# A chunked attention with two dense layers behind it: loads with 2 MB under way, one state sum moved, marks for two banks

## The chip, the cores and the metric

The kernel runs on one core of a Trainium2 chip. The metric is the device time of one execution in microseconds (us). Names of engines: PE is TensorE's matmul side, PEld its weight loads, DVE is VectorE, ACT is ScalarE, POOL is GpSimd, SP is SyncE, which here only issues transfers. One profiled execution of the kernel before is shown; other executions were only timed.

## The reference

A linear attention with decay (2 batches, 8 heads, 768 positions in 12 blocks of 64, head size 64), a dense layer pair with a leaky rectifier (1536 tokens, 512 to 2048 to 512), and a second pair (512 to 1024 to 512) with a softmax-weighted activation and a layer norm.

```python
for b in range(12):                                   # blocks of 64
    intra = (q_b @ k_b.T * Dmask) @ v_b
    inter = (q_b * lam_pow) @ kv_state
    out_b = intra + inter
    kv_state = lam_block * kv_state + (k_b * rev_pow).T @ v_b
x = out                                               # (1536, 512)
h = x @ w_in;  x = maximum(0.01 * h, h) @ w_out
h = x @ w_in2; s = h * softmax(h)
return (layernorm(s) * g_ln) @ w_out2
```

## The kernel before

**Numbers.** Weights come as 8-byte words, 512 KB a tile of 128 x 512 (`raww`). ACT and DVE turn each into two fp32r parts, a high one and a low one (`wio`): `word_hi` and `word_lo` on ACT (L351, L355), `clamp`, `shift`, `join` on DVE (L361, L371, L380), `high` on ACT (L410), `low` on DVE (L429). A product of two such numbers is three matmuls: high by high, high by low, low by high.

**Stages.** A prologue does attention steps 0 to 3 for the first 512 tokens, in products of 64 x 64. Then 48 units follow, 16 for each of three blocks of 512 tokens. Unit u makes 128 hidden columns (`l1_mm`, L440, 12 matmuls of 512 columns into a bank `hps`), ACT and DVE split them (`l1_split`: L443, L446, and `glo` L448 on DVE), and `l2_mm` (L457, 12 matmuls) adds them to `acc` one unit later. During the first 16 units the weights of the units to come are loaded and converted, one pair (a tile of `w_in` and a tile of `w_out`) for each unit; n counts pairs from 0. Steps 4 to 11 of the attention stand inside units 7, 10, 12, 14, 17, 21, 25 and 29. The second layer pair ends the kernel.

**A step.** `scores_mm` (L197) and `scores_ev` (L205, `r` on DVE) make the masked scores, `xs_mm` (L251) and `xq_mm` (L265) the output, `state_mm` (L211) the new sum for the state into bank `kb` (= `aps[1]`), `state_ev` (L237, or four instructions at L226) adds it on DVE to the decayed state. `x_hi` (L300, ACT) and `x_lo` (L304, DVE) split a step's output into `xhi` and `xlo`, which `l1_mm` reads. Steps of the prologue have the other half of rows than steps 4 to 11 have. In step 3, `xq_mm` goes ahead of `xs_mm`; `see` writes to the bank and has ACT copy one column of it, and the first `xs_mm` of each batch waits for that copy.

**Order.** Each engine runs its instructions in the order in which the code writes them; a pass at the end of the kernel fixes that. SP issues the loads in that order too. `load` adds one more wait: with `limit` bytes under way or more, a load waits for an earlier one. `AHEAD` is 2 MB, `CALM` 1 MB.

Of the kernel before, what the change touches and what calls it, by code (L numbers as in the profile page):

```python
# [10 lines left out]
U32 = mybir.dt.uint32  # L11
# [5 lines left out]
P = 128  # L17
CH = 64
NPAIR = 4
NB = 2  # L20
NPRE = 4
# [3 lines left out]
AHEAD, CALM = 1 << 21, 1 << 20  # L25
# [3 lines left out]
NF = FF1 // P  # L29
# [15 lines left out]
def fused_kernel(ctx: ExitStack, tc: tile.TileContext, att, vt, tab, cst, w_in, w_out, w_in2, w_out2, out):  # L45
# [7 lines left out]
    pe, dve, act, pool, sync = nc.tensor, nc.vector, nc.scalar, nc.gpsimd, nc.sync  # L53
# [10 lines left out]
    aps = [pp.tile([P, 512], F32, name=f"aps{i}") for i in range(2)]  # L64
# [19 lines left out]
    def rows(h):  # L84

        return HALF[1 - h]

    def jrows(s, h):

        return HALF[h] if s < NPRE else HALF[1 - h]  # L90
# [5 lines left out]
    def at(bank, rows, b, pr):  # L96

        if isinstance(bank, tuple):
            return bank[b][rows, pr * CH : (pr + 1) * CH]
        return bank[rows, (b * NPAIR + pr) * CH : (b * NPAIR + pr + 1) * CH]  # L100
# [12 lines left out]
    def load(queue, out, in_, limit=AHEAD):  # L113

        size = 4
        for n in out.shape:
            size *= n
        ins = queue.dma_start(out=out, in_=in_).ins
        ahead = size
        for before, n in reversed(flight):  # L120
            ahead += n
            if ahead > limit:
                tc.add_manual_dep(ins, before.name, SYNC, reason="bytes under way")
                break
        flight.append((ins, size))
# [67 lines left out]
    def scores_mm(s, bank, b, pr):  # L193
        q, k = (qk_t[s][:, :, 0], qk_t[s][:, :, 1]) if s >= NPRE else ld[s][0:2]
        for h in range(2):
            d = rows(h)
            pe.matmul(at(bank, jrows(s, h), b, pr), k[d, b, pr], q[d, b, pr], start=True, stop=True)  # L197
# [41 lines left out]
    LASTPRE, seen, mark = NPRE - 1, {}, tabs[:, 0:NB]  # L239

    def see(s, b):
        c = (b * NPAIR + NPAIR) * CH - 1
        bank = (aps, hps)[b][0]
        scores_mm(s, bank, b, NPAIR - 1)
        seen[b] = act.copy(mark[:, b : b + 1], bank[:, c : c + 1]).ins

    def xs_mm(s, bank, b, pr):
# [27 lines left out]
    def each_pair(*groups):  # L275

        for pr in range(NPAIR):
            for mm, s, bank, b in groups:
                mm(s, bank, b, pr)

    def alone(mm, s, bank):
        for b in range(NB):
            each_pair((mm, s, bank, b))

    def both(mm, s, bank, mm2, s2, bank2):
        for b in range(NB):
            each_pair((mm, s, bank, b), *([(mm2, s2, bank2, b)] if s2 < NS else []))

    def step(s, xbank, kbank, rbank):

        both(xs_mm, s, xbank, state_mm, s if s < NS - 1 else NS, kbank)
        both(xq_mm, s, xbank, scores_mm, s + 1, rbank)
# [5 lines left out]
    def x_hi(s, bank):  # L298
        for src, dst in parts(bank, x_place(s, xhi)):
            act.copy(dst, src)  # L300

    def x_lo(s, bank):
        for src, dst, hi in parts(bank, x_place(s, xlo), x_place(s, xhi)):
            dve.tensor_tensor(dst, src, hi.bitcast(F32), op=ALU.subtract)  # L304
# [8 lines left out]
    def whole(n):  # L313

        return IN if n == 0 else OUT if n == NF else BOTH

    def load_weights(n, halves=None):
        if n >= len(order):
            return
        kind, f = order[n]  # L320
        if n not in raws:
            if n == NF:
                raws[n] = tmp.tile([P, 1, 512, 2], U32, tag="s", name="rawl")
            else:
                raws[n] = wp.tile([P, 2, 512, 2], U32, tag="w", name="raww")
        t = raws[n]
        if kind == "a":
            load(sync, out=t.rearrange("p h a b -> p (h a b)"), in_=w_in2[f].bitcast(U32))
            return
        halves = halves or whole(n)  # L330
        for i in range(halves.start, halves.stop):
            src = w_out2[f + i] if kind == "b" else w_out[f - 1] if i else w_in[f]
            load(sync, out=t[:, 0 if n == NF else i].rearrange("p a b -> p (a b)"), in_=src.bitcast(U32), limit=AHEAD if n + i < 2 else CALM // 2 if n == 1 else CALM)

    def of(n, halves):

# [38 lines left out]
    def join(n, halves=None):  # L375
        if n >= len(order):
            return
        raw, x = of(n, halves)
        xu = x.bitcast(U32)
        dve.scalar_tensor_tensor(xu, xu, 0x80000000, raw[:, :, 0], op0=ALU.bitwise_and, op1=ALU.bitwise_or)  # L380
# [19 lines left out]
    def high(n, halves=None):  # L400
        if n >= len(order):
            return
        kind, f = order[n]
        halves = halves or whole(n)
        t, x = pieces(n), xs_t[n]
        if kind == "b":
            for i in range(2):
                act.activation(t[:, 0, i], x[:, i], AF.Copy, scale=gln[:, f + i : f + i + 1])
        else:
            act.copy(t[:, 0, halves], x[:, halves])  # L410
# [23 lines left out]
    def l1_mm(u, bank):  # L434
        b, f = u
        w = win_t[f].rearrange("p s (k c) -> p s k c", k=KD)
        groups = ((0, xhi), (1, xhi), (0, xlo)) if u == (0, 0) else ((0, xhi), (0, xlo), (1, xhi))
        terms = [(s, k, x) for s, x in groups for k in range(KD)]
        for i, (s, k, x) in enumerate(terms):
            pe.matmul(bank, w[:, s, k], x[b][:, k], start=(i == 0), stop=(i == len(terms) - 1))  # L440
# [136 lines left out]
    c1 = nc.const_aps.tensor(1.0, (P, 1), BF16)  # L577
# [3 lines left out]
    def busy(n):  # L581
        for _ in range(n):
            pe.matmul(aps[0], c1.to_broadcast([P, P]), c1.to_broadcast([P, 512]), start=True, stop=True)
# [29 lines left out]
    xb, sb, kb = acc[0:2], acc[2:4], aps[1]  # L613
# [47 lines left out]
    x3 = (xb[1], hps[1])  # L661
    for b in range(NB):
        each_pair((xq_mm, 3, x3, b))
        see(3, b)
    join(1, IN)
    x_lo(2, xb[0])
    both(xs_mm, 3, x3, state_mm, 3, kb)
    busy(1)
    x_hi(3, x3)
    high(1, IN)  # L670
    x_lo(3, x3)
# [42 lines left out]
    for i, u in enumerate(items[1:], 1):  # L714
        bank = hps[i % 2]
        s = step_at.get(i)
        spare = hps[(i + 1) % 2]
        if i > 1:
            if i == 5:
                alone(scores_mm, NPRE, aps[0])  # L720
            l1_mm(u, bank)
            if s is not None:
                step(s, aps[0], aps[1], spare)
        if i == 2:
            join(3, IN)
            high(3, IN)
            clamp(3, OUT)
            low(3, IN)
            shift(3, OUT)
            l1_split(u, bank)  # L730
            words(4, IN)
            join(3, OUT)
            high(3, OUT)
            clamp(4, IN)
            shift(4, IN)
            low(3, OUT)
            words(4, OUT)
            join(4, IN)
            high(4, IN)
            clamp(4, OUT)  # L740
            shift(4, OUT)
            low(4, IN)
            word_hi(5)
            join(4, OUT)
            word_lo(5)
        elif i == len(items) - 1:
            h2_norm(1, second=lambda: l1_split(u, bank))
        elif i > 2:
            part = OUT if i == 3 else None
            high(pair_at(i, 1), part)  # L750
            clamp(pair_at(i, 2))
            shift(pair_at(i, 2))
            low(pair_at(i, 1), part)
            l1_split(u, bank)
            if s is not None:
                scores_ev(s + 1, spare)
            if i == 6:
                scores_ev(NPRE, aps[0])
                scale_q(NPRE, pool)
                scale_k(NPRE, act)  # L760
            if s is not None:
                state_ev(s, aps[1])
                x_hi(s, aps[0])
                x_lo(s, aps[0])
                load_kv(s + 1)
                load_qk(s + 2)
                scale_q(s + 1, pool)
                decay_state(s + 1, pool)
            if i - 1 in step_at:
                scale_k(step_at[i - 1] + 1, act)  # L770
            join(pair_at(i, 2))
            if i == 4:
                state_ev(NPRE - 1, kb)
            words(pair_at(i, 3))
        load_weights(pair_at(i, 5))
        if i == 2:
            load_kv(NPRE)
            load(sync, out=fix, in_=cst)
            load_qk(NPRE + 1)
        if i == len(items) - 3:  # L780
            h2_norm(0)
            ln_turn(0, on_act=())
        l2_mm(items[i - 1])
        if items[i - 1][1] == NF - 1:
            l2_split(items[i - 1][0])
        if i in h2_after:
            h2_mm(h2_after[i])
# [84 lines left out]
```

## Time and profile before

| | us |
|---|---|
| median of 3 timed executions | 445.64 |
| lowest, highest of them | 443.67, 447.14 |
| the profiled execution's own time | 448.04 |
| its span, first to last instruction | 446.3 |
| PE busy, DVE busy, ACT busy | 435.1, 266.6, 196.1 |

The span is what the rows count in. The profiled execution's own time is 1.7 above it, and 2.4 above the median of the timed ones. Busy time of PE counts matmuls that overlap once.

### The profile page before, as it was taken

The numbers are of one execution on the slowest core, as the hardware profiler recorded it, in microseconds if no ns is written. First come the engines' busy times: TensorE is split into PE (matmuls) and PEld (weight loads), VectorE is DVE, ScalarE is ACT, GpSimd is POOL, SyncE is SP. The second block draws the span as 40 slices with busy tenths as digits, with TensorE's granted clock in tenths as the row PEclk, the third lists the DMA queues.
The fourth block names the chain that finished last, engine by engine and source line by source line (L and its number), as shares of the span: only waits on it lengthen the run. The fifth ranks groups of instructions, "written<-read, shape, count | busy, mean of one in ns | idle before, by whom it ended". The sixth has DMA issues, their size and how long they took to land.

```text
span 446.3 us, 8024 instructions
## 1 busy us (share of the span) xinstructions
PE 435.1 (97%) x3270; PEld 358.0 (80%) x3272; DVE 266.6 (60%) x423; ACT 196.1 (44%) x332; POOL 31.4 (7%) x38
## 2 busy tenths in 40 slices
PE   9779998999999999999999999999999999999996
PEld 4668887888888888888888888888888888888886
DVE  4769989999632121211132888707779877777640
ACT  3558976977452232221244778612423322222221
POOL 0600102022202020100000000000000000000000
PEclk9989999999999999999999999999999999999999
DMA  8757877864303030100015552000112222222111
GB/s 286 288 195 237 242 255 239 262 189 144 96 2 96 0 95 1 48 1 0 1 51 198 209 196 101 0 1 7 41 34 62 95 76 73 75 73 74 58 47 47
DMA packets 23699, 46.85 MB, mean 105 GB/s; under 512 B 4336, under 2 KB 12016, under 8 KB 23152
## 3 DMA queue, kind: packets, MB, share of 16 engines
q1 hardware_dynamic: 21792, 44.78, 30.9%
q10 hardware_dynamic: 1872, 1.58, 1.3%
q8 instruction: 25, 0.41, 0.4%
q14 instruction: 10, 0.08, 0.1%
HBM read 37.95 MB, written 3.15 MB: 92 GB/s over the span
## 4 chain that ended last, share of the span: by engine, by line
PE 83%; ACT 0%; issue 0%; DVE 0%
PE acc L457 25%; PE hps L440 24%; PE acc L569 15%; PE aps L477 6%; PE hps L477 5%; PE acc L477 4%; PE aps L251 1%; PE aps L265 1%; PE hps L197 0%; PE aps L211 0%; PE aps L537 0%; PE acc L537 0%; ACT osb L572 0%; DVE state L226 0%
## 5 line engine op out<-in xcount | busy, mean ns | idle before, releaser
L440 PE MATMUL hps<-xhi,wio 128*128 128x512 f32 x384 | 104.3, 394 | 1.6 <-DVE r L205 1.2
L448 DVE TENSOR_TENSOR glo<-hps,ghi 128x512 fp32r<-128x512 f32 x48 | 33.1, 690 | 111.8 <-ACT ghi L446 111.7
L457 PE MATMUL acc<-ghi,wio 128*128 128x512 f32 x384 | 95.9, 392 | 0.0
L440 PEld LDWEIGHTS hps<-xhi,wio 128*128 128x128 f32 x384 | 72.9, 191 | 17.1 <-ACT raww L355 1.5
L457 PEld LDWEIGHTS acc<-ghi,wio 128*128 128x128 f32 x384 | 71.4, 188 | 15.1
L443 ACT ACTIVATE hps<-hps 128x512 f32<-128x512 f32 x48 | 28.0, 584 | 105.7 <-PE hps L440 105.7
L569 PE MATMUL acc<-wb,ln 128*128 128x512 f32 (+1 forms) x312 | 67.6, 373 | 0.0
L569 PEld LDWEIGHTS acc<-wb,ln 128*128 128x128 f32 x312 | 55.3, 188 | 10.2
L440 PE MATMUL hps<-xlo,wio 128*128 128x512 f32 x192 | 51.3, 389 | 0.0
L457 PE MATMUL acc<-glo,wio 128*128 128x512 f32 x192 | 51.3, 389 | 0.0
L440 PEld LDWEIGHTS hps<-xlo,wio 128*128 128x128 f32 x192 | 36.0, 188 | 7.6
L457 PEld LDWEIGHTS acc<-glo,wio 128*128 128x128 f32 x192 | 36.0, 188 | 7.5
L380 DVE SCALAR_TENSOR_TENSOR x<-x,raww 128x1024 uint32<-128x1024 uint32 (+1 forms) x28 | 31.8, 1134 | 0.1
L351 ACT ACTIVATE x<-raww 128x1024 f32<-128x1024 f32 (+1 forms) x28 | 27.9, 996 | 8.5 <-DMA raww<-in_w_in_dram 5.2
L371 DVE SCALAR_TENSOR_TENSOR raww<-x,raww 128x1024 uint32<-128x1024 uint32 (+1 forms) x28 | 29.6, 1056 | 3.3 <-ACT raww L355 1.0
L446 ACT CAST ghi<-hps 128x512 fp32r<-128x512 f32 x48 | 28.2, 587 | 1.5
L355 ACT ACTIVATE raww<-raww 128x1024 uint32<-128x1024 uint16 (+1 forms) x28 | 28.1, 1003 | 0.0
L429 DVE TENSOR_TENSOR wio<-x,wio 128x1024 fp32r<-128x1024 f32 (+1 forms) x21 | 22.0, 1049 | 1.8 <-ACT wio L410 1.7
L510 POOL TENSOR_TENSOR small<-small,nhalf 128x1 f32<-128x1 f32 x12 | 6.6, 549 | 234.5 <-DVE small L509 234.5
L410 ACT CAST wio<-x 128x1024 fp32r<-128x1024 f32 (+1 forms) x21 | 17.8, 847 | 11.1 <-DVE x L380 11.1
L572 ACT COPY osb<-acc 128x512 f32<-128x512 f32 (+1 forms) x13 | 7.2, 554 | 32.0 <-PE acc L569 19.5
L166 POOL TENSOR_TENSOR qk<-qk,qpow 128x512 f32<-128x512 f32 x8 | 10.8, 1345 | 143.4 <-PE hps L197 109.0
(115 smaller groups left out, 496.1 us busy)
## 6 DMA issues: line engine op xcount, KB each, us to landing
raww<-in_w_out_dram SPq DMA_DIRECT2D x23, 512.0 KB, 4.2
raww<-in_w_in_dram SPq DMA_DIRECT2D x16, 512.0 KB, 4.4
qk<-in_att_dram SPq DMA_DIRECT2D x8, 512.0 KB, 4.6
raww<-in_w_in_dram SPq DMA_DIRECT2D x4, 1024.0 KB, 4.8
lt<-e SPq DMA_DIRECT2D x124, 32.0 KB, 1.8
out_dram<-osb SPq DMA_DIRECT2D x11, 256.0 KB, 2.2
ldw<-in_att_dram SPq DMA_DIRECT2D x7, 384.0 KB, 5.2
kv<-in_att_dram SPq DMA_DIRECT2D x16, 128.0 KB, 3.4
```

The costliest lines, as they stand in the source:

```text
L351: act.activation(x, raw[:, :, 1].bitcast(F32), AF.Copy, scale=HI_SCALE)
L355: act.activation(raw[:, :, 0], raw.bitcast(U16)[:, :, 1], AF.Copy, scale=LO_SCALE)
L371: dve.scalar_tensor_tensor(raw[:, :, 0], x.bitcast(U32), 3, raw[:, :, 0], op0=ALU.logical_shift_left, op1=ALU.bitwise_or)
L380: dve.scalar_tensor_tensor(xu, xu, 0x80000000, raw[:, :, 0], op0=ALU.bitwise_and, op1=ALU.bitwise_or)
L429: dve.tensor_tensor(t[:, 1, halves], x[:, halves], t[:, 0, halves].bitcast(F32), op=ALU.subtract)
L440: pe.matmul(bank, w[:, s, k], x[b][:, k], start=(i == 0), stop=(i == len(terms) - 1))
L443: act.activation(bank, bank, AF.Prelu, alpha=0.01)
L446: act.copy(ghi, bank)
L448: dve.tensor_tensor(glo, bank, ghi.bitcast(F32), op=ALU.subtract)
L457: pe.matmul(acc[m], w[:, s, m], g, start=(f == 0 and first), stop=(f == NF - 1 and last))
L477: pe.matmul(bank, x[b][:, k, o : o + P], w2_t["a", k, half][:, s], start=(i == 0), stop=(i == len(terms) - 1),)
L569: pe.matmul(po[:, 0:n], x[:, k], w2_t["b", k][:, s, cols], start=(i == 0), stop=(i == len(terms) - 1))
```

## The change

Three things change, and nothing in the order of the loads.

Weight loads from pair 3 on (the fourth) have the limit of 2 MB in place of 1 MB; pair 1 keeps 2 MB for its first tile and 512 KB for its second, pair 2 keeps 1 MB.

`state_mm` of step 3 leaves the prologue, where it alternated with `xs_mm`, and alternates with `scores_mm` of step 4 in unit 5; its `state_ev` goes from unit 4's row of the loop to unit 6's. A filler matmul (`busy(1)`) behind it goes.

`see` writes its mark by one bf16 matmul of 64 columns of ones, where it computed two products of scores before; the copied column is another one.

```diff
     def see(s, b):
-        c = (b * NPAIR + NPAIR) * CH - 1
+        c = CH - 1
         bank = (aps, hps)[b][0]
-        scores_mm(s, bank, b, NPAIR - 1)
+        pe.matmul(bank[:, 0:CH], c1.to_broadcast([P, P]), c1.to_broadcast([P, CH]), start=True, stop=True)
         seen[b] = act.copy(mark[:, b : b + 1], bank[:, c : c + 1]).ins
...
-            load(sync, out=t[:, 0 if n == NF else i].rearrange("p a b -> p (a b)"), in_=src.bitcast(U32), limit=AHEAD if n + i < 2 else CALM // 2 if n == 1 else CALM)
+            load(sync, out=t[:, 0 if n == NF else i].rearrange("p a b -> p (a b)"), in_=src.bitcast(U32), limit=CALM // 2 if n == 1 and i else CALM if n == 2 else AHEAD)
...
     x_lo(2, xb[0])
-    both(xs_mm, 3, x3, state_mm, 3, kb)
-    busy(1)
+    alone(xs_mm, 3, x3)
     x_hi(3, x3)
...
             if i == 5:
-                alone(scores_mm, NPRE, aps[0])
+                both(scores_mm, NPRE, aps[0], state_mm, NPRE - 1, kb)
...
-            if i == 4:
+            if i == 6:
                 state_ev(NPRE - 1, kb)
```

On PE, at the end of the prologue, the 16 state products (`aps_86<-ldw`) and the filler went from between step 3's output products (`acc_80` and `hps_84` `<-r,ldw`) and the first matmuls of unit 0:

```order
-L251 MATMUL hps_84<-r,ldw 64x64 x2
-L211 MATMUL aps_86<-ldw 64x64 x2
-L583 LDWEIGHTS const-bfloat16-1.0
-L583 MATMUL aps_85<-const-bfloat16-1.0 128x512
+L244 LDWEIGHTS const-bfloat16-1.0
+L244 MATMUL hps_83<-const-bfloat16-1.0 128x64
+L251 MATMUL acc_80<-r,ldw 64x64 x8
+L251 MATMUL hps_84<-r,ldw 64x64 x8
 L440 MATMUL hps_83<-xhi_95,wio 128x512 x8
```

Unit 0 now follows step 3's 16 output products at once; the products that left stand in unit 5.

On DVE, in unit 6, the addition of step 3's state comes behind `join` (L380) of pair 8, where it came behind that of pair 6 before:

```order
 L205 TENSOR_TENSOR r<-aps_85,dmask 128x512
 L380 SCALAR_TENSOR_TENSOR x<-x,raww 128x1024
+L237 TENSOR_TENSOR state<-aps_86,sd 128x512
 L361 TENSOR_SCALAR x<-x 128x1024
 L371 SCALAR_TENSOR_TENSOR raww<-x,raww 128x1024
```

It is now the last thing on DVE ahead of unit 7, whose step 4 reads that state.

On SP, from the second tile of pair 2 (`raww_141`) over pair 3 (`raww_144`) and step 4's `qk` to pair 4 (`raww_149`); the names in brackets are semaphores of earlier transfers. Before:

```order
L118 DMA raww_141<-in_w_out_dram 128x1024 [waits DMAHW7_49]
L118 DMA raww_144<-in_w_in_dram 128x1024 [waits DMAHW2_49,DMAHW0_49]
L118 DMA raww_144<-in_w_out_dram 128x1024 [waits DMAHW3_49,DMAHW1_49]
L118 DMA qk_147<-in_att_dram 128x2x512 [waits DMAHW4_49]
L118 DMA raww_149<-in_w_in_dram 128x1024 [waits DMAHW5_49,DMAHW3_49]
```

And after the change:

```order
L118 DMA raww_141<-in_w_out_dram 128x1024 [waits DMAHW7_49]
L118 DMA raww_144<-in_w_in_dram 128x1024 [waits DMAHW2_49]
L118 DMA raww_144<-in_w_out_dram 128x1024 [waits DMAHW3_49]
L118 DMA qk_147<-in_att_dram 128x2x512 [waits DMAHW4_49,DMAHW0_49]
L118 DMA raww_149<-in_w_in_dram 128x1024 [waits DMAHW5_49,DMAHW1_49]
```

The loads stand in one order in both; what moved is which landing each waits for, two transfers further back.

## Rows read from the trace of the kernel before

**Rows 1.** The page: the chain's shares by engine, and the DMA rate by fortieths.

```profile
PE 83%; ACT 0%; issue 0%; DVE 0%
...
GB/s 286 288 195 237 242 255 239 262 189 144 96 2 96 0 95 1 48 1 0 1 51 198 209 196 101 0 1 7 41 34 62 95 76 73 75 73 74 58 47 47
```

**Rows 2.** Waits of PE: who waited for whom, us in total, times, longest.

```profile
PE aps L211 <- issue: 2.4, 1, 2.4
PE hps L440 <- DVE r L205: 1.2, 1, 1.2
```

**Rows 3.** Stretches: PE, PEld, DVE, ACT, POOL busy (x instructions), clock, DMA, GB/s.

```profile
13.62:19.00 5.38, 3.11 (x128) 2.97 (x127) 3.63 (x6) 3.75 (x11) 4.39 (x4) 1.00 0.61 238
19.00:25.20 6.20, 3.53 (x127) 3.40 (x128) 4.50 (x7) 2.21 (x6) 0.61 (x1) 1.00 0.82 264
...
26.30:29.70 3.40, 3.14 (x7) 2.49 (x8) 2.90 (x6) 3.07 (x7) 0.00 (x0) 0.50 0.79 270
...
26.56:72.72 46.16, 46.16 (x340) 37.58 (x340) 42.53 (x58) 38.98 (x59) 2.98 (x2) 0.97 0.73 234
73.87:110.00 36.13, 36.13 (x396) 29.96 (x397) 34.58 (x41) 27.11 (x40) 5.79 (x5) 1.00 0.70 209
```

**Rows 4.** Timeline of PE, prologue to unit 8: start, length, instruction, wait.

```profile
16.34 0.27 PE L251 MATMUL acc<-r,ldw 64*64 64x64 f32 x2
...
17.34 0.40 PE L197 MATMUL acc<-ldw 64*64 64x64 f32 x7
19.47 0.97 PE L197 MATMUL acc<-ldw 64*64 64x64 f32 x25 [1.73 <-issue]
...
25.40 0.21 PE L211 MATMUL aps<-ldw 64*64 64x64 f32 x1 [2.40 <-issue]
...
26.56 3.55 PE L440 MATMUL hps<-xhi,wio 128*128 128x512 f32 x8 [0.42 <-ACT xhi L300]
29.94 1.09 PE L440 MATMUL hps<-xlo,wio 128*128 128x512 f32 x4
30.87 1.09 PE L440 MATMUL hps<-xhi,wio 128*128 128x512 f32 x4
...
52.74 1.15 PE L197 MATMUL aps<-qk 64*64 64x64 f32 x32
...
67.67 0.27 PE L251 MATMUL aps<-r,kv 64*64 64x64 f32 x2
...
69.70 2.11 PE L457 MATMUL acc<-ghi,wio 128*128 128x512 f32 x8
...
73.87 1.15 PE L440 MATMUL hps<-xhi,wio 128*128 128x512 f32 x4 [1.16 <-DVE r L205]
```

**Rows 5.** Timeline of ACT.

```profile
26.13 0.37 ACT L300 CAST xhi<-hps 128x256 fp32r<-128x256 f32 x1 [2.79 <-PE hps L251]
...
31.13 0.58 ACT L443 ACTIVATE hps<-hps 128x512 f32<-128x512 f32 x1 [0.83 <-PE hps L440]
...
61.46 1.14 ACT L351 ACTIVATE x<-raww 128x1024 f32<-128x1024 f32 x1 [2.70 <-DMA raww<-in_w_out_dram]
```

**Rows 6.** Timeline of DVE.

```profile
32.36 0.69 DVE L448 TENSOR_TENSOR glo<-hps,ghi 128x512 fp32r<-128x512 f32 x1 [0.99 <-ACT ghi L446]
...
62.64 0.70 DVE L361 TENSOR_SCALAR x<-x 128x1024 f32<-128x1024 f32 x1 [0.74 <-ACT x L351]
63.67 1.23 DVE L371 SCALAR_TENSOR_TENSOR raww<-x,raww 128x1024 uint32<-128x1024 uint32 x1 [0.34 <-ACT raww L355]
...
67.14 1.22 DVE L380 SCALAR_TENSOR_TENSOR x<-x,raww 128x1024 uint32<-128x1024 uint32 x1
...
73.05 0.68 DVE L205 TENSOR_TENSOR r<-hps,dmask 128x512 f32<-128x512 f32 x1
```

**Rows 7.** The tile of step 3's state on DVE, in unit 4's row.

```profile
L237 DVE TENSOR_TENSOR state<-aps,sd x1: 677/677/677, 56.4 to 56.4; 128x512 f32<-128x512 f32 x1
```

**Rows 8.** Timeline of SP: the issue of pair 3's first tile.

```profile
23.62 0.33 SPq L118 DMA_DIRECT2D raww<-in_w_in_dram  x1
```

## The prediction

> **What bounds the kernel now.** I began with the chain that ended last: 83% of the span lies on PE and next to nothing on ACT, DVE or issue [rows 1]. The stretches then say where PE has no gap: from 26.56, the first matmul of unit 0, to 72.72 it is busy 46.16 of 46.16 us, and from 73.87 to 110.00 again 36.13 of 36.13 [rows 3]. So ahead of 110 an edit can move the end in three ways: unit 0 starts earlier, the wait between 72.72 and 73.87 gets shorter, or a stretch of the clock changes. The list of PE's waits names them [rows 2]: 2.4 us with no releaser ahead of a state product in the prologue, and 1.2 us for DVE's `r` ahead of unit 8.
>
> The first is the more telling. On the timeline PE stops at 17.74 (17.34 and 0.40) until 19.47, and at 23.00 until 25.40, with nothing that it waits for [rows 4]. Between the ends of one pause and the start of the next stand 128 matmuls and as many weight loads, give or take one [rows 3]: 256 instructions. Pauses that stand a fixed count of instructions apart, whatever the instructions are, are waits for code. I treat them so: the pause belongs to the 256th instruction, and the block of code behind it came 5.93 us after PE had gone on from the last pause (19.47 to 25.40). A 64 x 64 product in fp32 is two matmuls there, so the narrow products of the prologue use code up fast: 32 products in 1.0 us (16.34 to 17.34).
>
> The pause costs more than itself. PE had done almost nothing from 23.00 to 25.40, and from 26.30 to 29.70 the granted clock is 0.50, that is 1.2 GHz in place of 2.4 [rows 3]: the first eight matmuls of unit 0 take 3.38 us (26.56 to 29.94), the next four 0.93 [rows 4].
>
> Next I asked what sets the second wait. DVE's `r` ran at 73.05 [rows 6], and DVE is busy 42.53 of 46.16 us up to there [rows 3]: it is nearly the bound itself. Its waits on the way are 0.99 ahead of `glo` of unit 0, where ACT had waited 0.83 for the slow matmuls, and 0.74 and 0.34 ahead of pair 8's conversion, where ACT had waited 2.70 for that pair's second tile [rows 5, 6].
>
> **The change, part by part.** *The state products leave the prologue.* From the pause's end at 19.47 the code now runs 25 matmuls of step 3's scores, 32 and 32 of `xq_mm` for steps 2 and 3, 2 marks, 32 of `xs_mm`: 123. The 128th is the fifth of unit 0. Ahead of unit 0 the pause is gone. `x_hi` of step 3's second batch ran at 26.13, having waited 2.79 for these products [rows 5]; less 2.40, and less about 0.1 for the marks, which are one matmul each for four, it runs at 23.6, and unit 0 starts at 26.56 - 2.5 = 24.05. Worth 2.5. The 16 products take nothing else with them: alternating with the output products they ran beside those (32 in 1.0 us, where 16 alone take about 1.1 at 52.74) [rows 4]. The filler stood in `x_hi`'s time, so it was free and stays so.
>
> *In unit 5* they alternate with the scores of step 4. Bounds: nothing, by the alternating row, to 1.15, the length of such 16 alone [rows 4]. I take 0, the row that has the same pairing.
>
> *The pause in its new place.* Five matmuls at 0.23 end at 25.2; if the block comes when it came, at 25.40, PE stands 0.2. The other seven end at 27.0, at the full clock, since PE now works in most of the stretch in which it stood still. Before, those twelve ended at 30.87. PE is 3.87 ahead.
>
> The Trainium skill, "Runtime: NRT & Kernel Launch", section "Instruction fetch mechanics", has engines read code in blocks of 256 instructions, the next while the last runs, and calls the cost of crossing "mostly hidden". The count agrees with the trace, the cost does not: 1.73 and 2.40 us stand open here. By the page the pause would be something else and might stay; the rival for that is below.
>
> *DVE and ACT.* Both run up to unit 0's split in the order that they had, 2.5 earlier. ACT would be free for it at 31.13 - 0.83 - 2.5 = 27.8, and PE has ended at 27.0, so the 0.83 goes and `glo` comes 3.3 earlier, at 29.05.
>
> *2 MB under way.* The wait at 61.46 was for the second tile of pair 8. From pair 3's first tile to that one SP issues twelve tiles of 0.52 MB, `qk` twice, `kv` and a small table: 7.9 MB. The first two fortieths, with 2 MB under way, moved 286 and 288 GB/s, the fourth to eighth 237 to 262 [rows 1]. From 23.62, where pair 3 was issued [rows 8] (it goes a little earlier now), 7.9 MB are through at 51.3 by the first rate and at 57 by the lowest of the second. ACT wants the tile at 58.76 - 3.3 = 55.5. By the first rate nobody waits; by the second ACT waits 1.5, less than the 1.62 that DVE did not feel of the 2.70. So DVE's 0.74 + 0.34 = 1.08 goes in both. The ends: 0 to 1.08; I take 1.08. Durations on ACT and DVE I leave as they are.
>
> *The addition of step 3's state* is 0.68 on DVE [rows 7] and stands ahead of `r` of unit 7 in both kernels, so the sum up to `r` is the same. But step 4's state products need its bank and its result. `join` of pair 8 ran at 67.14 [rows 6]; 4.4 earlier it ends at about 63.9 and the addition at 64.5, while PE reaches step 4 at 67.67 - 3.87 = 63.8. PE stands 0.7 there, with the rest of the step and `l2_mm` of unit 6 queued behind. The step itself takes 2.03 (67.67 to 69.70) [rows 4]. That is covered: PE has to wait for `r` behind them anyway. Without that cover it costs 0.7. On POOL and SP the move issues nothing. The tile with step 3's `k` and `v` is held until unit 5; the load that takes it over is that of pair 12, seven pairs on.
>
> *The sum.* DVE's `r` of unit 7 comes 3.3 + 1.08 = 4.4 earlier, and unit 8 starts at 69.5 in place of 73.87. PE alone would be there at 72.72 - 3.87 = 68.8, or 69.5 with the wait in step 4, so DVE still decides, by little, and half of the 1.16 stays. Behind unit 8 PE and DVE stand to each other as before, with the loads not later. 448.04 - 4.4 = 443.6 for an execution like the profiled one.
>
> That one lies above all three timed ones (443.67 to 447.14), which differ by 3.5 with nothing changed. What varies is most likely what this sum removes: a faster execution may not have had the slow clock or the wait for pair 8. So I count 2.5 for the pause in full, and half of the other 1.9 against the median: 445.64 - 3.45 = 442.2. The measurement tells about 1% from no change, which is 441.2 on this side and 450.1 on the other.
>
> **The rivals.**
>
> *The pause comes back inside unit 0.* The third block is read under more loads than before. If it comes at 26.9, 7.4 us after the last pause, PE stands 1.7 again and the clock may fall again: seven matmuls at 0.42 end at 29.85, `glo` (1.49 behind, as 30.87 to 32.36) at 31.3, a gain of 1.0, and 1.08 with it: 445.64 - 2.1 = 443.6, between 443.1 and 445. For it: 5.93 us was under 264 GB/s, and the five matmuls cover only 1.2. Against: the loads that come early are issued behind 22, and the block was due before they weigh much.
>
> *More than the sum.* If DVE drops out of the way, PE alone gives 3.87 + 1.16 = 5.0: 440.6. For it: DVE is only 0.7 behind PE in the sum. Against: step 4's new wait for the addition.
>
> *Slower: code behind 2 MB of loads.* If the block's time grows with the bytes under way, PE stands in unit 0 far longer. It decides from 29.0 on: seven matmuls at 0.42 end at 31.95, `glo` at 33.44, which eats the 1.08. With twice 5.93 the block comes at 31.3 and the gain turns into a loss of 2.3: 447.9. Over 1% takes 33.5. Against: only the third block is in reach; the next falls 128 wide matmuls later.
> The Trainium skill, "DMA: Bandwidth & Descriptors", section "Queues, rings and completion order", has each DMA engine take turns between queues packet by packet; by that code would not stand behind all the loads. No row here shows single packets.
>
> *It does not do what it says.* If the pauses are not code, the pause stays where it is in the program's time, and only 0 to 1.08 is gained: 444.6 to 445.6.
>
> **How the numbers follow.** Forecast 0.44 (441.2 to 443.1 for gains of 2.5 to 4.4), pause back 0.26, more 0.17, no effect 0.07, slower 0.06. The range runs from 440.6, PE alone, to 445.0, the end of the first rival; outside lie half of "more", most of "no effect" and "slower", less than 0.2. Faster by over 1%: "more" and the edge of the forecast, 0.30. Slower by over 1%: 0.04 (half of that rival and what I do not see). Within 1%: 0.66.
>
> **What would show it.** Right: no pause ahead of step 3's `x_hi`; unit 0 at about 24.0; a pause, short, ahead of its fifth matmul; granted clock 1.00 through unit 0; no wait of ACT for a weight tile behind 30; unit 8 at about 69.5. Wrong: a pause of over 1 us in unit 0, a stretch at 0.50 there, unit 8 later than 71.5, or a wait of over 1 us in step 4.

## The result, and the profile after

The changed kernel takes 442.36 us (median of 16, 441.44 to 443.50), the kernel before 446.08 in the same series (16, 443.67 to 449.08): a ratio of 0.9916, 95% interval 0.9895 to 0.9936. The forecast was 442.2, and the measured time lies in the range. The spread shrank too, from 5.4 to 2.1.

The profiled execution took 441.71, its span 439.9. PE's timeline, to be held against [rows 4]:

```profile
17.94 0.97 PE L197 MATMUL acc<-ldw 64*64 64x64 f32 x25 [1.10 <-issue]
18.69 1.61 PE L265 MATMUL acc<-qs,state 64*64 64x64 f32 x48
20.24 0.20 PE L244 MATMUL aps<-const-bfloat16-1.0 128*128 128x64 bf16 x1
...
21.63 0.63 PE L251 MATMUL hps<-r,ldw 64*64 64x64 f32 x16
...
22.74 2.11 PE L440 MATMUL hps<-xhi,wio 128*128 128x512 f32 x8 [0.47 <-ACT xhi L300]
24.68 1.07 PE L440 MATMUL hps<-xlo,wio 128*128 128x512 f32 x4
25.59 1.07 PE L440 MATMUL hps<-xhi,wio 128*128 128x512 f32 x4
...
64.75 2.11 PE L457 MATMUL acc<-ghi,wio 128*128 128x512 f32 x8
...
67.60 1.07 PE L440 MATMUL hps<-xhi,wio 128*128 128x512 f32 x4
```

Ahead of unit 0 PE waits only 0.47 for `xhi`, as it waited 0.42 before; there is no pause without a releaser there, none inside unit 0, and no wait ahead of unit 8. The stretches (columns as in [rows 3]) say the same, and that step 4 (62.36 to 64.75) got longer:

```profile
22.74:67.60 44.86, 44.81 (x372) 36.93 (x373) 43.28 (x65) 39.78 (x59) 4.05 (x2) 1.00 0.76 270
67.60:110.00 42.40, 42.40 (x543) 35.18 (x542) 39.03 (x45) 31.62 (x48) 5.97 (x6) 1.00 0.51 178
...
62.36:64.75 2.39, 2.35 (x130) 2.17 (x129) 2.30 (x4) 1.83 (x3) 0.00 (x0) 1.00 0.02 7
```

DVE, to be held against [rows 6]: `glo` of unit 0, the addition that moved, `low` of pair 8 and `r` of unit 7, with no wait on the way for pair 8:

```profile
27.73 0.69 DVE L448 TENSOR_TENSOR glo<-hps,ghi 128x512 fp32r<-128x512 f32 x1
...
61.96 0.68 DVE L237 TENSOR_TENSOR state<-aps,sd 128x512 f32<-128x512 f32 x1
...
64.47 1.22 DVE L429 TENSOR_TENSOR wio<-x,wio 128x1024 fp32r<-128x1024 f32 x1
...
66.21 0.68 DVE L205 TENSOR_TENSOR r<-hps,dmask 128x512 f32<-128x512 f32 x1
```

The DMA rate by fortieths, to be held against [rows 1]: the third to fifth moved 305 to 358 where they had moved 195 to 242. Behind that the loads came in bursts (74, 337, 84).

```profile
GB/s 295 282 305 349 358 74 337 84 219 71 97 52 47 13 85 0 49 1 0 1 95 192 191 191 97 0 1 16 33 43 81 81 76 73 72 75 73 55 48 48
```

How much earlier the loads run is read from SP. It issues the second tile of pair 8, the one that ACT waited 2.70 for [rows 5], 13.2 us earlier. Before and after:

```profile
56.66 0.33 SPq L118 DMA_DIRECT2D raww<-in_w_out_dram  x1
```

```profile
43.45 0.43 SPq L118 DMA_DIRECT2D raww<-in_w_out_dram  x1
```

So PE is the bound from 22.74 to 110, and I take the time of an execution as the start of unit 0 and a constant: 441.71 - 22.74 = 419.0. Three kernels below have profiled executions with no wait behind the start of unit 0 too: 4 MB 442.24 - 23.39 = 418.9, the state back in the prologue 441.07 - 22.50 = 418.6, the second one of the loads alone 444.50 - 25.95 = 418.6. With 418.8 I account for each profiled execution: start, plus waits of PE, plus slow clock. Over all fourteen of them, with those waits and the slow clock taken off, the constant comes to between 418.5 and 419.6, so it does not resolve differences of under 1 us. The profiled execution before comes to 26.56 + 418.8 + 1.46 (twelve matmuls in 4.31 in place of 2.85) + 1.16 = 448.0, and took 448.04.

### The profile page after: what moved, and what is told of

Read it like the earlier page. It is cut to its first block, busy times and chain, and to the rows that moved or that the text cites. A ratio compares the mean times of both kernels' runs of the same rounds, so it can differ in the third digit from the quotient of the medians.

```text
span 439.9 us, 8004 instructions
## 1 busy us (share of the span) xinstructions
PE 433.2 (98%) x3264; PEld 357.2 (81%) x3265; DVE 265.9 (60%) x423; ACT 196.0 (45%) x332; POOL 32.3 (7%) x38
## 4 chain that ended last, share of the span: by engine, by line
PE 96%; DMA 3%; issue 0%; SPq 0%; ACT 0%
PE acc L457 30%; PE hps L440 30%; PE acc L569 15%; PE aps L477 6%; PE hps L477 5%; PE acc L477 4%; PE aps L251 2%; DMA ldw<-in_att_dram 1%; DMA raww<-in_w_in_dram 1%; PE aps L265 1%; PE aps L211 1%; PE acc L265 1%; PE hps L197 0%; PE acc L197 0%; PE acc L251 0%
## 5 line engine op out<-in xcount | busy, mean ns | idle before, releaser
L440 PE MATMUL hps<-xhi,wio 128*128 128x512 f32 x384 | 102.7, 390 | 0.5 <-ACT xhi L300 0.5
L440 PEld LDWEIGHTS hps<-xhi,wio 128*128 128x128 f32 x384 | 71.9, 188 | 15.5 <-ACT xhi L300 0.6
L440 PE MATMUL hps<-xlo,wio 128*128 128x512 f32 x192 | 51.3, 389 | 0.0
L457 PE MATMUL acc<-glo,wio 128*128 128x512 f32 x192 | 51.3, 389 | 0.0
L380 DVE SCALAR_TENSOR_TENSOR x<-x,raww 128x1024 uint32<-128x1024 uint32 (+1 forms) x28 | 32.2, 1150 | 0.1
L166 POOL TENSOR_TENSOR qk<-qk,qpow 128x512 f32<-128x512 f32 x8 | 11.9, 1482 | 139.0 <-PE hps L197 109.5
L429 DVE TENSOR_TENSOR wio<-x,wio 128x1024 fp32r<-128x1024 f32 (+1 forms) x21 | 21.1, 1003 | 1.5 <-ACT wio L410 1.5
```

The lines of the kernel that those rows point to most:

```text
L429: dve.tensor_tensor(t[:, 1, halves], x[:, halves], t[:, 0, halves].bitcast(F32), op=ALU.subtract)
L457: pe.matmul(acc[m], w[:, s, m], g, start=(f == 0 and first), stop=(f == NF - 1 and last))
```

## The experiments

Ratios are against the kernel before on the same chip, by all timed executions and not by the medians alone; the medians of the kernel before there were 444.79 (first four), 446.47 (next four) and 445.51 (last four). The whole change was not timed in the series of the first four, so where their medians are held against its 442.36, the chips may differ.

**The loads alone.**

```diff
-    load(..., limit=AHEAD if n + i < 2 else CALM // 2 if n == 1 else CALM)
+    load(..., limit=CALM // 2 if n == 1 and i else CALM if n == 2 else AHEAD)
```

> Only the limits of the loads are changed; state products and marks stay as in the kernel before. Theory (the gain is the pause ahead of unit 0 and, with it, DVE's shorter way to unit 8, where the loads only take away a wait of 1.08): the pause ahead of a state product stays, 1.5 to 2.5 us; ACT has no wait for a weight tile behind 30 us; the wait of PE ahead of unit 8 is under 0.4; the time falls by 0.5 to 1.3 us, ratio 0.997 to 0.999. Rival (the loads are the gain, the moved products hide nothing that counts): the time falls by 3 us or more, ratio 0.993 or less, as in the changed kernel.

Measured: 442.27 (12, 441.14 to 446.25), ratio 0.9954 (0.9927 to 0.9980). The profiled execution (446.09) is the second slowest of the twelve. PE's timeline there:

```profile
24.73 0.21 PE L211 MATMUL aps<-ldw 64*64 64x64 f32 x1 [2.38 <-issue]
25.89 3.55 PE L440 MATMUL hps<-xhi,wio 128*128 128x512 f32 x8 [0.42 <-ACT xhi L300]
29.23 1.27 PE L440 MATMUL hps<-xlo,wio 128*128 128x512 f32 x4
```

The pause stays, as the theory said, and no tile is waited for. But the median fell by 2.5, twice what I had allowed, to about that of the changed kernel. The theory's sizes fail; the rival's bound (0.993) lies in the interval, but is missed by the ratio and by the medians (0.9943).

**The moves alone.** The edits of state products, addition and marks; limits as before.

> State products, addition and marks as in the changed kernel; the limits of the loads as in the kernel before. Theory: no pause between step 3's output products and unit 0, unit 0 starts 4.8 us (4.5 to 5.3) after PE goes on from the pause in step 2's scores, but the loads come no earlier, ACT waits longer than 2.70 for pair 8 or a pair near it, and PE waits 1 to 4 us ahead of unit 8 or in the units around; the time falls by 0 to 2.5 us, ratio 0.994 to 1.000. Rival (the pause is the whole gain): the ratio is that of the changed kernel, 0.992. Rival (the loads are the gain): ratio 1.000.

Measured: 445.16 (12, 443.01 to 446.50), ratio 0.9991 (0.9968 to 1.0015): no gain. The profiled execution is the fastest of the twelve, with unit 0 at 23.74 and no pause ahead of it; PE waits only 0.38 behind that:

```profile
23.74 2.11 PE L440 MATMUL hps<-xhi,wio 128*128 128x512 f32 x8 [0.47 <-ACT xhi L300]
64.08 0.27 PE L211 MATMUL aps<-kv 64*64 64x64 f32 x2 [0.38 <-ACT raww L355]
```

So the pause goes, and the median does not follow.

**State products back in the prologue**, with the loads and the marks.

```diff
-    alone(xs_mm, 3, x3)
+    both(xs_mm, 3, x3, state_mm, 3, kb)
+    busy(1)
...
-                both(scores_mm, NPRE, aps[0], state_mm, NPRE - 1, kb)
+                alone(scores_mm, NPRE, aps[0])
...
-            if i == 6:
+            if i == 4:
```

> The changed kernel with the state products, the filler and the addition of step 3 where they were before; limits of loads and marks are those of the changed kernel. Theory (a pause stands each 256 PE instructions): the marks save 6 matmuls, so the pause falls among the last of the alternating products of step 3's second batch, still ahead of unit 0; the time is that of the loads alone, ratio 0.996 to 0.999, and not that of the changed kernel. Rival (the marks are what helps): 0.992.

Measured: 442.11 (8, 441.06 to 443.82), ratio 0.9934 (0.9905 to 0.9963). The profiled execution, the second fastest, has no pause without a releaser ahead of unit 0:

```profile
17.70 0.97 PE L197 MATMUL acc<-ldw 64*64 64x64 f32 x25 [1.16 <-issue]
22.50 2.11 PE L440 MATMUL hps<-xhi,wio 128*128 128x512 f32 x8 [0.46 <-ACT xhi L300]
```

The expected pause did not come, and the ratio is nearer to the rival's 0.992 than to the theory's 0.996 to 0.999. The loads alone have nearly the same median, so it does not speak for the marks; that they add something is neither shown nor excluded (the intervals overlap).

**The old marks in the changed kernel.**

```diff
-        c = CH - 1
+        c = (b * NPAIR + NPAIR) * CH - 1
         bank = (aps, hps)[b][0]
-        pe.matmul(bank[:, 0:CH], c1.to_broadcast([P, P]), c1.to_broadcast([P, CH]), start=True, stop=True)
+        scores_mm(s, bank, b, NPAIR - 1)
```

> The changed kernel with the marks of the kernel before (two products of scores each, 8 matmuls in place of 2). Theory of the count: from the end of the pause in step 2's scores it is now 129 matmuls to unit 0, so the block ends one matmul ahead of unit 0, and a pause, where there is one, stands ahead of the last output product or the first matmul of unit 0; against the changed kernel up to 1.7 us are lost (five matmuls of cover and what they hide), the ratio lies between 0.992 and 0.997. Rival (pauses are no matter of the count): no pause there, and the ratio is 0.992 within 0.001.

Measured: 442.24 (12, 441.39 to 445.77), ratio 0.9947 (0.9927 to 0.9967). The profiled execution (445.77, the slowest) has the pause where the count puts it, ahead of the last two of the 129 matmuls:

```profile
21.91 0.68 PE L251 MATMUL hps<-r,ldw 64*64 64x64 f32 x14
24.80 0.27 PE L251 MATMUL hps<-r,ldw 64*64 64x64 f32 x2 [2.21 <-issue]
25.53 2.67 PE L440 MATMUL hps<-xhi,wio 128*128 128x512 f32 x8 [0.46 <-ACT xhi L300]
```

Pauses are a matter of the count: that held. That each execution has one did not: ten of these twelve took 441.39 to 442.59.

So the question became what an ordinary execution of the kernel before is like. Two more were profiled. The "old theory" below is that the pause stands in each execution, the "new" one that in most the loads are late instead.

> The kernel before, unchanged, to see an ordinary execution. Of 31 timed executions of it five show a granted clock of 0.996 (445.4 to 447.7 us), as the profiled one did, the others 0.999 or 1.000 (median 444.76). New theory (the pause with the slow clock is in one of six executions; in the others the loads are what lags): no stretch at 0.50, the pause ahead of unit 0 under 0.7 us, unit 0 at 22.5 to 24, ACT waiting 2 to 6 us in all for weight tiles between 30 and 65, PE waiting 1 to 4 us in all up to unit 9. Old theory (the pause is in each execution): a pause of 2 us or more and a slow stretch.

Measured: 448.15. PE's timeline, the clock and ACT's waits for tiles:

```profile
22.78 0.21 PE L211 MATMUL aps<-ldw 64*64 64x64 f32 x1 [1.01 <-issue]
...
47.95 3.23 PE L457 MATMUL acc<-ghi,wio 128*128 128x512 f32 x8 [1.92 <-ACT ghi L446]
```

The clock behind that wait (columns as in [rows 3]):

```profile
48.00:52.00 4.00, 4.00 (x11) 3.14 (x12) 3.62 (x5) 3.42 (x4) 0.00 (x0) 0.58 0.88 268
```

ACT:

```profile
44.14 1.12 ACT L351 ACTIVATE x<-raww 128x1024 f32<-128x1024 f32 x1 [2.43 <-DMA raww<-in_w_out_dram]
48.58 1.18 ACT L351 ACTIVATE x<-raww 128x1024 f32<-128x1024 f32 x1 [0.68 <-DMA raww<-in_w_out_dram]
53.84 1.15 ACT L351 ACTIVATE x<-raww 128x1024 f32<-128x1024 f32 x1 [0.98 <-DMA raww<-in_w_out_dram]
61.54 1.12 ACT L351 ACTIVATE x<-raww 128x1024 f32<-128x1024 f32 x1 [3.46 <-DMA raww<-in_w_out_dram]
```

The same time as the profiled execution's 448.04, by another way. Unit 0 starts at 23.94, 2.6 sooner. But ACT waits for the second tiles of pairs 5, 6, 7 and 8 (and 0.51 for pair 4's), 8.1 in all; PE waits 1.92 for unit 3's `ghi` and 1.3 for `r` ahead of unit 8, and behind the first of these the clock falls (0.58 from 48 to 52). 23.94 + 418.8 + 3.2 and some 1.5 of slow clock (an estimate, by the 1.46 above) are 447.4; 0.7 I can't place.

> The kernel before once more, for the same reason, since one execution tells little of what varies. New theory: as above, with the waits of ACT for weight tiles and PE's waits up to unit 9 there again; the time less the start of unit 0 agrees with the other look within 1.5 us when neither has a slow stretch. Old theory: a pause of 2 us or more ahead of unit 0.

Measured: 445.86. PE's timeline:

```profile
24.48 0.21 PE L211 MATMUL aps<-ldw 64*64 64x64 f32 x1 [2.11 <-issue]
25.64 3.19 PE L440 MATMUL hps<-xhi,wio 128*128 128x512 f32 x8
...
30.08 1.09 PE L440 MATMUL hps<-xhi,wio 128*128 128x512 f32 x4
```

A pause of 2.11, unit 0 at 25.64, its first twelve matmuls in 4.44, and no wait for a tile: 25.64 + 418.8 + 1.6 = 446.0. Here the old theory's picture is right, and the new one's is not. Two things vary by themselves in this kernel: the start of unit 0 (23.94 to 26.56 in three profiled executions) and the pace of the loads (pair 8's second tile was issued at 52.60 here, at 56.96 in the one above and at 56.66 in the first). An execution waits for tiles where the loads are late against unit 0.

**2 MB from pair 8 on only.**

```diff
-    load(..., limit=AHEAD if n + i < 2 else CALM // 2 if n == 1 else CALM)
+    load(..., limit=AHEAD if n + i < 2 or n >= 8 else CALM // 2 if n == 1 else CALM)
```

> The kernel before with the limit of 2 MB from pair 8 on only (pairs 3 to 7 keep 1 MB). If the lag is made at pair 8, behind the loads of keys, values, the table and the queries: about all of what the loads give, ratio 0.994 to 0.996. If it is made pair by pair from pair 3 on: less than half of it, ratio 0.998 to 1.001.

Measured: 445.68 (12, 443.25 to 448.17), ratio 0.9981 (0.9956 to 1.0006). By the median less than half of what the loads alone gave on their chip (0.8 of 2.5), which points to a lag made among pairs 3 to 7; the intervals of the two ratios overlap, so it is not settled. The profiled execution (445.99) has the long pause, 2.40, and ACT waits 1.03 for one tile.

**4 MB from pair 3 on** (`2 * AHEAD` in place of the last `AHEAD`).

> The changed kernel with 4 MB in place of 2 MB from pair 3 on. New theory: the loads are ahead of their readers with 2 MB already, so nothing is gained: the median of the changed kernel, 442.4, within 0.7, ratio 0.992 to 0.996. Rival (more loads in the way of the code): a pause in unit 0 in some executions, granted clock 0.996 there, and a median higher by 1 us or more.

Measured: 442.45 (6, 441.46 to 443.37), ratio 0.9914 (0.9885 to 0.9942). More than 2 MB gave nothing.

**The addition one unit earlier** (`if i == 5` in place of 6).

> The changed kernel with the addition of step 3's state in unit 5's row, one unit earlier, so that it is done when PE reaches step 4. In the changed kernel step 4 takes 2.39 us against 2.03 before, 0.37 of it ahead of the first state product. If that wait is PE's only one there: step 4 in 2.0 to 2.1 us, the median 0.2 to 0.5 us below the changed kernel's 442.36, ratio 0.990 to 0.994. Rival (DVE is late by then and PE waits for r ahead of unit 8 as much longer): no change in the time, a wait of 0.3 or more ahead of unit 8.

Measured: 441.56 (6, 440.83 to 442.78), ratio 0.9906 (0.9880 to 0.9931). In the profiled execution (442.78, the slowest) step 4 takes about 2.1, and nothing waits ahead of unit 8, so the rival falls. PE waits 0.60 for unit 1's `ghi` there, behind a wait of ACT of 1.37 for a weight tile at 24.75: the new limits do not keep every early tile in time. The median is 0.8 lower than the changed kernel's, but from another chip and six executions, and the interval holds the changed kernel's ratio. Taken with 0.60 off, this execution has 419.3 behind the start of unit 0, no less than the changed kernel's 419.0. That this version beats the changed kernel is not shown.

**2 MB for pairs 1 and 2 too** (`limit=AHEAD` for all).

> The changed kernel with 2 MB for pairs 1 and 2 as well, so that loads are under way all through the prologue. Rival of the record (code comes later when more loads are under way): the block ahead of unit 0 or the one in step 2's scores comes 6 us or more after PE went on, a pause of 1 us or more stands in unit 0 or grows by as much in the prologue, median 443.4 or more. Theory: the code takes its turn among the loads, the pauses grow by less than 0.5, median within 0.7 of the changed kernel's 442.36.

Measured: 441.78 (7, 441.31 to 444.78), ratio 0.9929 (0.9902 to 0.9957). In the profiled execution (441.78) the pause in step 2's scores was 0.51, none stood between it and unit 0 or inside unit 0, and unit 0 started at 22.27: there, more loads under way did not hold up the code. One of the seven executions (444.78) has a mean clock of 0.996 and was not profiled.

**The moves, a second profiled execution.**

> The moves without the loads once more: the look at it was at its fastest execution (443.01, median 445.16), which lacks what the median shows. Theory: in an ordinary execution unit 0 starts at 22.5 to 24 with no pause ahead of it, ACT waits 2 us or more in all for second tiles of pairs 4 to 8, PE waits 1 to 4 us up to unit 9. Rival: the time goes elsewhere, with no wait for a tile.

Measured: 445.21, the median of that kernel. PE's timeline, and the longest of ACT's four waits for a tile (6.3 in all):

```profile
22.26 2.11 PE L440 MATMUL hps<-xhi,wio 128*128 128x512 f32 x8 [0.47 <-ACT xhi L300]
45.02 2.11 PE L457 MATMUL acc<-ghi,wio 128*128 128x512 f32 x8 [0.71 <-ACT ghi L446]
61.78 1.19 PE L440 MATMUL hps<-xhi,wio 128*128 128x512 f32 x4 [1.52 <-ACT wio L410]
66.23 0.27 PE L211 MATMUL aps<-kv 64*64 64x64 f32 x2 [1.17 <-ACT raww L355]
```

```profile
58.65 1.12 ACT L351 ACTIVATE x<-raww 128x1024 f32<-128x1024 f32 x1 [4.14 <-DMA raww<-in_w_out_dram]
```

That is where the moves' gain goes in this execution: unit 0 starts 4.3 sooner than in the profiled execution before, but pair 8's second tile is issued only 2.7 sooner (53.99), and PE waits 3.4 in three places. 22.26 + 418.8 + 3.4 are 444.5; 0.7 I can't place.

**The loads, a second profiled execution.**

> The loads without the moves once more: its look was at one of two executions in twelve with a slow clock (446.09, median 442.27). Theory: the time is the start of unit 0 and 418.8 us (as in the changed kernel, 22.74 and 441.71), and 1.5 more with a slow stretch; so in an execution near the median unit 0 starts at 23 to 24, the pause ahead of it is under 0.7 us, and no wait for a tile stands behind 30.

Measured: 444.50, again above that kernel's median. PE's timeline and its clock:

```profile
19.69 1.65 PE L197 MATMUL acc<-ldw 64*64 64x64 f32 x25 [2.28 <-issue]
...
24.79 0.21 PE L211 MATMUL aps<-ldw 64*64 64x64 f32 x1 [0.16 <-issue]
25.95 2.09 PE L440 MATMUL hps<-xhi,wio 128*128 128x512 f32 x8 [0.42 <-ACT xhi L300]
```

```profile
19.69:23.10 3.41, 3.41 (x68) 3.41 (x70) 1.74 (x4) 0.07 (x1) 0.00 (x0) 0.54 0.88 318
```

The constant held (418.6) and no tile is waited for. The long pause stood in step 2's scores this time, the slow clock came behind it, and the pause ahead of unit 0 was 0.16. So no profiled execution of the loads alone lies near that kernel's median.

## Why the prediction came out, point by point

**The time and the range** were right, the way there only in part. The step that failed is the one to the median: "So I count 2.5 for the pause in full, and half of the other 1.9". It is the other way round. The loads alone take the median down by 2.5 (444.79 to 442.27), where I had given them 0.5; the moves alone leave it (445.16), where I had given them 2.5 and more. Two wrong sizes made a sum that came out right by luck. And the parts measured do not fill it: 2.5 and nothing, against 3.7 for the whole change in another series. By the ratios (0.9954 and 0.9916) the moves may give up to some 0.4% on top of the loads; the intervals overlap, and no series timed both.

**The wait for loads** was mis-sized because I read one execution. In it unit 0 was late, so most tiles were in time and DVE felt 1.08 [rows 6]. Where unit 0 starts 2.6 sooner and the loads do not, ACT waits 8.1 for tiles, and PE 3.2. A start of unit 0 that is made earlier, by the moves or by chance, is worth nothing in the median while the loads keep their old pace; single executions keep some of it (the moves alone at 443.01, with loads that were early). My sum had both parts, but added them; they hang together. The rate itself I had nearly right: by the first rate the 7.9 MB were to be through at 51.3, and the tile that ends them had landed by 49.8 (issued at 43.45) and was not waited for.

**The pause is code, by the count:** the count is confirmed by the old marks (2.21 ahead of the last two of 129) and by six profiled executions of five kernels with all the moves, which show none ahead of unit 0. That what comes late is code is argued from the count; no row shows the fetch. That it is always there: wrong. With the state products in the prologue the profiled executions have 2.40, 1.01, 2.11, 2.38, 0.16, 0.00 and 2.40 in its place. The short pause forecast ahead of unit 0's fifth matmul did not come. The timed executions tell how often the long pause stands: of the fourteen profiled ones, the seven with a mean granted clock of 0.995 or 0.996 each have a stand of PE (idle time) of 1.92 to 2.40 and a slow stretch behind it, the other seven have neither. Of the 60 timed executions of the kernel before in the experiments, 18 have such a mean. So most of them lack what I counted in full.

**What the moves give** beside the loads is a shorter tail, as far as it can be told. Of 33 executions with the new limits but the products or marks as before, six took over 444; of 35 with all the moves, one. The mean clock agrees: 18 of 60 before and six of those 33 have a slow one, and one of 48 with all the moves, old limits or new. Which of the two edits does it is not told: one of the eight with the state products back has it, and five of the 25 with the old marks. The medians (442.27, 442.11, 442.24 against 442.36) do not differ.

**DVE's `r` ahead of unit 8.** I had some 0.6 of wait left, half of the 1.16; there is none. PE is the bound there, which is the mechanism of the rival "more than the sum", though the median stayed above that rival's 440.6. `r` ran at 66.21, and from `glo` of unit 0 it is 38.5 in place of 40.7 [rows 6]: 1.08 of that is the wait for pair 8, nearly all the rest one instruction, `low` of pair 8, in 1.22 (64.47) where it had taken 2.31 before:

```profile
70.21 2.31 DVE L429 TENSOR_TENSOR wio<-x,wio 128x1024 fp32r<-128x1024 f32 x1
```

POOL's product runs beside it in both, for 1.95 after and 1.53 before; why now POOL is the one that gets longer, no run tells.

**Step 4's new wait**: 0.36 in place of 0.7 (2.39 against 2.03 [rows 4]), and the cover that I gave it is gone with the wait for `r`, so it lies in the open. Unit 5's 16 products: from the end of `l2_mm` of unit 3 to unit 5's first wide matmul it is 1.18 (47.35 to 48.53) with them, and was 1.17 (52.65 to 53.82) without; no cost.

**Unit 0** started at 22.74, not 24.05: PE went on at 17.94, not 19.47 [rows 4], and from there it took 4.80 (forecast 4.58). Nothing that I know of in the change reaches that far back; the pauses of the prologue vary by themselves (the one at this place has 0.51 to 2.28 over the fourteen).

**The rivals.** No pause came back inside unit 0 in any profiled execution, and neither 4 MB nor 2 MB for all pairs brought one. The block ahead of unit 0 came as late with the new limits alone (5.92 behind the last pause, 18.81 to 24.73) as before (5.93), so nothing speaks for "code behind 2 MB of loads". The sentence of the Trainium skill ("DMA: Bandwidth & Descriptors", section "Queues, rings and completion order") on DMA engines that take turns between queues agrees with that, though no row shows single packets. What the Trainium skill says of code that is read while the last block runs ("Runtime: NRT & Kernel Launch", section "Instruction fetch mechanics") fits the good executions and not the 2.1 to 2.4 of the others.

**Open.** Why a block of code comes 4.55 us after PE goes on in one execution (18.23 to 22.78) and 6.20 in another (18.60 to 24.80) isn't settled, nor why the profiled executions have more of the long pauses than the timed ones do (all three of the kernel before have a slow stretch, and both of the loads alone are among the four of its 13 executions above 444). Profiling may lengthen them; no run tells. Nor is it told why the pace of the loads varies under the old limits.

## What to carry to other kernels

A profile is one execution: list the spread of the timed ones beside it, and if it lies above them all, find out what it has that they lack before you put a price on its largest stall. Two stalls in a row on the same path are no sum: when the first goes, a later one that was hidden behind it grows, so try each edit alone and both together. In a kernel whose tail is a steady run of matmuls, the start of that run and a constant account for each execution, here to within 1 us; what is left over points at the waits. And the mean clock of every timed execution tells how often a stall with a slow stretch behind it happens, where one trace tells only that it can.

## What the runs showed of the hardware that I had not expected

Each of the seven stands of PE of 1.92 to 2.40 us in the fourteen profiled executions was followed by a granted clock near half, wherever it stood: 0.50 from 26.30 behind a pause of 2.40 [rows 3], 0.54 from 19.69 behind 2.28, 0.58 from 48 to 52 behind a wait of 1.92 in the middle of the dense part. Where it fell on unit 0, its first twelve matmuls took 4.17 to 4.45 in place of 2.85, that is 1.3 to 1.6 us more. Behind the stands of 1.10 (changed kernel) and 1.73 (kernel before) in step 2's scores it did not fall.

Loads with 1 MB under way moved 195 to 262 GB/s in the third to eighth fortieth [rows 1], with 2 MB in the changed kernel 305 to 358 in the third to fifth. The conversions did not get longer by it: `word_hi` of 128 x 1024 on ACT takes 1.12 to 1.19 in all profiled executions.
